# A decode attention block: half of the value products shared between VectorE and ScalarE, and a weight load cut by rows

## Chip, cores and metric

The kernel runs on one core of a Trainium2 chip. The metric is device time in microseconds for one execution. Before the change three runs gave 1308.16, 1308.84 and 1309.59 us, median 1308.84.

A core has TensorE (PE, matrix products), VectorE (DVE), ScalarE (ACT), GpSimd (POOL) and SyncE (SP, which here issues the loads). Each engine works through its own instructions in the order of the built program and waits on semaphores for the others. Sixteen DMA engines move data between memory and the core.

## The reference

One token for each of two sequences goes through an attention block with a cache and a dense block, in float32: B = 2, H = 32 heads, 8192 cached positions, head width 128, D = 512, hidden width F = 1792.

```python
# A: attention with cache
q = (x @ wq) -> [B, H, 1, 128]
scores = einsum("bhqd,bhkd->bhqk", q, k_cache) * 128**-0.5
p = softmax(scores)
o = einsum("bhqk,bhkd->bhqd", p, v_cache)
A = o.reshape(B, 1, H * 128) @ wo
# B: dense block
r = max(x @ w1 + b1, 0);  Bx = (r * r) @ w2 + b2
# whole
x = A_x
h = x + A(layernorm(x))
out = h + B(layernorm(h))
```

The two caches are 512 MiB of the 561 MB that the kernel reads.

## The kernel before

There are 64 pairs of head and sequence, here called heads 0 to 63. Each has a row of 16384 floats for each of the 128 partitions: 8192 of keys, 8192 of values, 8 MB in all. The host lays them out so that the four quarters of the positions (2048 each, `CS`) lie beside one another, and the values of a head are four columns `e` of 2048 positions (`NH = 4`), each partition holding one quarter and one of 32 widths.

`ring` in the core's memory has three slots of one head each. SyncE loads head i + 3 into the slot that head i leaves (`load_kv`). Slot 0 holds the query weights first and, at the end, the output weights `WO` (the first 16 of 32 heads of them where the keys were, the rest where the values were); slot 1 holds the dense weights `W1` and `W2` at the end.

For each head i, in this order:

- `scores` (L157 to L165): TensorE multiplies the query with the keys, 16 products of 512 columns (two passes each, so x32 in the profile), into four banks of the accumulator memory, a tile `s` of 128 x 2048. VectorE takes the negated maximum of each row into `NM` (L164).
- `exponentials` (L167 to L169): ScalarE writes exp(s - max) over `s` and sums it into `LS`.
- `weighted` (L171 to L174): for each of the four value columns one VectorE instruction multiplies the column with `s`, in place, and sums the products into `AC`. Each is followed by a short read of the accumulator.

The loop (L236 to L258) then issues the loads. Heads come in three groups, 0 to 31, 32 to 61, and 62 and 63. When a group's heads are done, `weigh` (L176 to L192) brings their maxima and sums together (L181, L183, L185, L186, L188, L189, L191), `join` (L194 to L201) gives the attention outputs `OT`, `project` (L203 to L211) multiplies them with `WO` (L207) and copies the rows by ScalarE (L210), and `add_rows` (L213 to L217) adds them to `hT`. Group 0 is joined after head 60, group 1 after head 61.

The end of the load stream is: head 61, the first half of `WO`, head 62 in two halves, head 63's keys, the second half of `WO`, head 63's values in pieces of 1 MB (three) and 512 KB (two), `W1` in four loads, `W2` in five. A load uses one of eight completion semaphores in turn, so SyncE issues a load only when the one eight before it has landed.

After the loop, head 63's values are multiplied piece by piece as they land (L287 to L295), the last heads' share of the output is added through centred weights `woc` (L308), and the dense block follows: the hidden layer `hidden` in two halves (L315) around the variance (L321) and its root `rstd` (L117), a transpose, bias and squared maximum (L329 to L334), the second layer (L337), and the store. The instruction order of each engine comes out of a scheduler that takes the program text as its starting order; `issue_after` fixes a few places.

Of the kernel before, what the change touches and what calls it, by code (L numbers as in the profile page):

```python
# [9 lines left out]
AF = mybir.ActivationFunctionType  # L10
ALU = mybir.AluOpType
AX = mybir.AxisListType

B, H, SK, DH, D, F = 2, 32, 8192, 128, 512, 1792
P = 128
NQ = 4
CS = SK // NQ
NH = DH // 32
DB = D // P
# [6 lines left out]
BLK = 512  # L26
GROUPS = [(0, 16), (16, 31), (31, 32)]
W2_PIECES = [4, 4, 3, 2, 1]
EPS = 1e-5
SCALE = DH ** -0.5  # L30

# [2 lines left out]
def attention_block_kernel(ctx: ExitStack, tc: tile.TileContext, small, kvd, wqd, wod, w1d, w2d, out):  # L34
    nc = tc.nc
# [7 lines left out]
    def slot(i):  # L43
        return ring[:, (i + 1) % SLOTS if i < BH - 2 else i - BH + 3]
# [4 lines left out]
    def values(i):  # L49
        return slot(i)[:, HALF:].rearrange("p (e c) -> p e c", e=NH)  # L50

    WQ = ring[:, 0].rearrange("p (d c) -> p d c", d=DB)
    WO = ring[:, 0].rearrange("p (h c) -> p h c", h=H)
# [3 lines left out]
    def load_kv(i):  # L57
        nc.sync.dma_start(slot(i), kvd[i])  # L58

    def load_wo(a, b):  # L60
        nc.sync.dma_start(WO[:, a:b], wod[:, a:b])
# [14 lines left out]
    eps_t = consts.tile([P, 1], F32, name="eps_t")  # L76
    nc.vector.memset(eps_t, EPS)
    zero = consts.tile([P, 1], F32, name="zero")
# [30 lines left out]
    def squares(xc):  # L109
        sq = work.tile([P, DB, B], F32, name="sq")  # L110
        nc.vector.tensor_tensor(sq, xc, xc, op=ALU.mult)
        return summed(sq)

    def scale_of(pm):

        rstd = work.tile([P, B], F32, name="rstd")
        nc.scalar.activation(rstd, pm, AF.Sqrt, bias=eps_t, scale=1.0)  # L117
        nc.vector.reciprocal(rstd, rstd)
        return rstd
# [9 lines left out]
    rstd = scale_of(bk[3][:, B : 2 * B])  # L129
# [5 lines left out]
    for k in range(2):  # L135
        for d in range(DB):
            for j in range(NQ):
                n = k * NQ + j
                nc.tensor.matmul(bk[k][32 * j : 32 * j + B, :], xn[:, d, :], WQ[:, d, n * BLK : (n + 1) * BLK],  # L139
                                 start=(d == 0), stop=(d == DB - 1))  # L140
# [13 lines left out]
    AC = consts.tile([P, BH, NH], F32, name="AC")  # L154
    OT = consts.tile([P, BH], F32, name="OT")

    def scores(i):  # L157

        s, bk = banks()
        for n in range(CS // BLK):  # L160
            for j in range(NQ):
                nc.tensor.matmul(bk[n][32 * j : 32 * j + 32, :], QR[:, i, :], keys(i)[:, j, n * BLK : (n + 1) * BLK],  # L162
                                 start=True, stop=True)
        nc.vector.tensor_reduce(NM[:, i : i + 1], s, axis=AX.X, op=ALU.max, negate=True)  # L164
        return s  # L165

    def exponentials(i, s):  # L167

        nc.scalar.activation(s, s, AF.Exp, bias=NM[:, i : i + 1], scale=1.0, accum_out=LS[:, i : i + 1])  # L169

    def weighted(i, s, e, lo, hi, acc, by=1.0):  # L171

        v = values(i)[:, e, lo:hi]
        return nc.vector.scalar_tensor_tensor(v, v, by, s[:, lo:hi], op0=ALU.mult, op1=ALU.mult, accum_out=acc)  # L174

    def weigh(a, b, pn, pl):  # L176

        nb = b - a
        pn = pn[:, : NQ * nb].rearrange("p (j i) -> p j i", j=NQ)
        for j in range(NQ):  # L180
            nc.tensor.matmul(pn[:, j], pick[:, j, :], NM[:, a:b], start=True, stop=True)  # L181
        gm = work.tile([P, BH], F32, name="gm")[:, :nb]
        nc.vector.tensor_reduce(gm, pn.rearrange("p j i -> p i j"), axis=AX.X, op=ALU.min)  # L183
        w = work.tile([P, BH], F32, name="w")[:, :nb]
        nc.vector.tensor_tensor(w, gm, NM[:, a:b], op=ALU.subtract)  # L185
        nc.scalar.activation(w, w, AF.Exp)  # L186
        lw = work.tile([P, BH], F32, name="lw")[:, :nb]
        nc.vector.tensor_tensor(lw, LS[:, a:b], w, op=ALU.mult)  # L188
        nc.tensor.matmul(pl[:, :nb], pick_all, lw, start=True, stop=True)  # L189
        rl = work.tile([P, BH], F32, name="rl")[:, :nb]  # L190
        nc.vector.reciprocal(rl, pl[:, :nb])  # L191
        return w, rl  # L192
# [26 lines left out]
    last = BH - 1  # L219
    g_at = [(a * B, b * B) for a, b in GROUPS]  # L220

    def group(n, project_now):

        a, b = g_at[n]
        _, bk = banks()
        w, rl = weigh(a, b, bk[0], bk[1])
        join(a, b, w, rl, bk[2])
        if project_now:
            clear(bk[3], D)
            add_rows(project(*GROUPS[n], bk[3]), bk[0])  # L230

    def load_half(i, half):
        cut = slice(half * HALF, (half + 1) * HALF)
        nc.sync.dma_start(slot(i)[:, cut], kvd[i][:, cut])

    for i in range(last):  # L236
        s = scores(i)
        exponentials(i, s)
        for e in range(NH):
            weighted(i, s, e, 0, CS, AC[:, i, e : e + 1])  # L240
        if i + 3 < last - 1:
            load_kv(i + 3)
        if i == last - 4:
            load_wo(0, H // 2)
        if i == last - 3:
            load_half(last - 1, 0)
            load_half(last - 1, 1)
            group(0, True)
        if i == last - 2:
            load_half(last, 0)  # L250
            load_wo(H // 2, H)
            for e in range(NH):
                n = 2 if e == NH - 1 else 1
                for k in range(n):
                    lo, hi = k * CS // n, (k + 1) * CS // n
                    at = HALF + e * CS
                    nc.sync.dma_start(values(last)[:, e, lo:hi], kvd[last][:, at + lo : at + hi])
            group(1, False)  # L258
# [3 lines left out]
    at = 0  # L262
    for n in W2_PIECES:
        nc.sync.dma_start(W2[:, at : at + n], w2d[:, at : at + n])
# [6 lines left out]
    with tc.issue_after(clear(o, P).ins):  # L271
        exponentials(last, sl)
    a, b = g_at[2]
    w, rl = weigh(a, b, sums[:, :64], sums[:, 64:128])
    nc.scalar.activation(warm, w[:, 0:1], AF.Sqrt)
    nc.vector.tensor_tensor(w, w, rl, op=ALU.mult)


    woc = work.tile([P, D], F32, name="woc")
# [19 lines left out]
        nc.tensor.matmul(po[at : at + 32, :B], fold, aw[:, :, e], start=(e < NH), stop=(e != NH - 1))  # L299
    with tc.issue_after(done.ins):  # L300
        nc.vector.tensor_copy(OT[:, a:b], po[:, :B])
    xc = work.tile([P, DB, B], F32, name="xc")
    with tc.issue_after(done.ins):
        nc.vector.tensor_tensor(xc, hT, pm[:, None, :].to_broadcast([P, DB, B]), op=ALU.subtract)
        nc.vector.tensor_tensor(hT, hT, b2T[:, :, None].to_broadcast([P, DB, B]), op=ALU.add)
    ph = sums[:, 256 : 256 + DB * B].rearrange("p (d b) -> p d b", b=B)
    for d in range(DB):
        nc.tensor.matmul(ph[:, d, :], woc[:, d * P : (d + 1) * P], OT[:, a:b], start=True, stop=True)  # L308
    nc.vector.tensor_tensor(xc, xc, ph, op=ALU.add)


    def hidden(ds):
        for d in ds:
            for j in range(NQ):
                mm = nc.tensor.matmul(y[32 * j : 32 * j + B, :], xc[:, d, :], W1[:, d, j * FQ : (j + 1) * FQ],  # L315
                                      start=(d == 0), stop=(d == DB - 1))
        return mm

    var = sums[:, 384 : 384 + B]
    with tc.issue_after(hidden(range(2)).ins):  # L320
        mm = nc.tensor.matmul(var, ones_d, squares(xc), start=True, stop=True)  # L321
    rstd = scale_of(var)
    with tc.issue_after(mm.ins):
        hidden(range(2, DB))
    for j in range(NQ):
        nc.tensor.matmul(o[32 * j : 32 * j + B, :], hT[:, j, :], ident, start=True, stop=False)  # L326
        nc.tensor.matmul(o[32 * j : 32 * j + B, :], OT[:, a:b], WO[:, H - 1, j * P : (j + 1) * P], start=False, stop=False)  # L327
# [7 lines left out]
    for m in range(FB):  # L335
        for j in range(NQ):
            nc.tensor.matmul(o[32 * j : 32 * j + B, :], a2[:, m, :], W2[:, m, j * P : (j + 1) * P],  # L337
                             start=False, stop=(m == FB - 1))
# [33 lines left out]
```

## Time and profile before

| | |
|---|---|
| median of three runs | 1308.84 us (1308.16 to 1309.59) |
| the profiled execution | 1310.04 us, span 1308.3 us |
| mean granted clock of TensorE | 0.643 |
| TensorE products busy | 417.7 us (32%) |
| VectorE busy | 728.9 us (56%) |
| ScalarE busy | 145.0 us (11%) |
| DMA | 561.44 MB in 12122 packets, mean 429 GB/s |
| issue to landing of a head's load, median | 38.8 us |

The span runs from the profiled execution's first instruction to its last; its own time is 1.7 us longer. The groups of instructions give line, engine, operation, output and inputs with shapes, count, busy time in us, mean duration in ns, and the idle time of the engine just before them with what ended most of it. The chain of waits follows back from the last instruction what released each step. Times in it and in the timeline are us from the span's start.

### The profile page before, as it was taken

The page shows a single profiled execution, that of the slowest core. Times are in us where ns is not written, and L with a number is a line of the kernel's source. Part 1 is how long each engine was busy: PE and PEld are TensorE (multiplying, and loading weights), DVE is VectorE, ACT ScalarE, POOL GpSimd, SP SyncE. Part 2 cuts the span into 40 slices and gives each one's busy share as a digit, 9 for nine tenths or more (in the row PEclk, how much of TensorE's full clock was granted, in tenths as well). Part 3 has the DMA queues.
Part 4 walks back from the last instruction along what each step waited for, and adds up shares of the span by engine and source line. Part 5 has one row for each costly group of instructions (what it writes and reads, how often), then busy time and mean ns, then how long its engine had stood idle before and what let it go on. Part 6 is the DMA issues. An engine that isn't in the chain of part 4 may idle for free.

```text
span 1308.3 us, 6011 instructions
## 1 busy us (share of the span) xinstructions
PE 417.7 (32%) x2438; PEld 114.7 (9%) x2438; DVE 728.9 (56%) x626; ACT 145.0 (11%) x152; POOL 0.7 (0%) x6
## 2 busy tenths in 40 slices
PE   2423223323323323322322332332332332332446
PEld 0100000000000000000000000000000000000113
DVE  0464665564565565565566466556456556556553
ACT  1111011011011011011101101101101101101111
POOL 0000000000000000000000000000000000000000
PEclk9666667566656666666656666756665665665766
DMA  9999999999999999999999999999999999999997
GB/s 417 417 447 425 439 433 431 441 425 443 425 439 423 441 429 435 433 435 432 433 431 435 430 437 431 435 431 433 431 437 429 437 429 437 428 439 429 426 426 313
DMA packets 12122, 561.44 MB, mean 429 GB/s; under 512 B 1472, under 2 KB 1600, under 8 KB 2752
## 3 DMA queue, kind: packets, MB, share of 16 engines
q1 hardware_dynamic: 11952, 561.06, 99.3%
q8 instruction: 19, 0.31, 0.1%
q14 instruction: 7, 0.06, 0.0%
q10 hardware_dynamic: 144, 0.01, 0.0%
HBM read 561.00 MB, written 0.07 MB: 429 GB/s over the span
## 4 chain that ended last, share of the span: by engine, by line
DMA 62%; DVE 20%; PE 12%; ACT 4%; another core or an unknown queue 1%; issue 1%; SPq 0%; ACTq 0%
DMA ring<-in_kvd 62%; DVE ring L174 16%; PE s L162 11%; DVE NM L164 4%; ACT s L169 4%; PE s L315 0%; PE s L337 0%; PE s L308 0%; DVE yT L329 0%; PE s L189 0%; PE s L321 0%; PE s L327 0%; SPq L58 0%; PE s L326 0%
## 5 line engine op out<-in xcount | busy, mean ns | idle before, releaser
L162 PE MATMUL s<-ring,QR 128*32 128x512 f32 x2048 | 373.1, 895 | 827.1 <-DMA ring<-in_kvd 718.9
L174 DVE SCALAR_TENSOR_TENSOR ring<-ring,s 128x2048 f32<-128x2048 f32 x252 | 561.5, 2284 | 133.6 <-ACT s L169 133.6
L164 DVE TENSOR_REDUCE NM<-s 128x1 f32<-128x2048 f32 x64 | 146.6, 2291 | 383.4 <-PE s L162 383.4
L169 ACT ACTIVATE s<-s,NM 128x2048 f32<-128x2048 f32 x64 | 124.3, 1942 | 1072.5 <-DVE NM L164 1072.5
L162 PEld LDWEIGHTS s<-ring,QR 128*32 128x32 f32 x2048 | 93.3, 156 | 1104.4 <-issue 1100.9
L174 DVE DVE_READ_ACCUMULATOR ring<-ring,s 128x1 f32 x252 | 20.9, 83 | 0.0
L99 DVE TENSOR_REDUCE part<-sm 128x2 f32<-128x8 f32 x1 | 0.2, 160 | 21.9 <-DMA sm<-in_small 21.9
L169 ACT ACTIVATION_READ_ACCUMULATOR s<-s,NM 128x1 f32 x64 | 12.3, 193 | 0.0
L139 PE MATMUL s<-ring,xn 128*2 128x512 f32 x64 | 9.5, 749 | 1.5 <-ACT rstd L117 0.8
L174 DVE SCALAR_TENSOR_TENSOR ring<-ring,w,s 128x2048 f32<-128x2048 f32 (+1 forms) x5 | 9.6, 1916 | 0.6 <-DMA ring<-in_kvd 0.4
L207 PE MATMUL s<-ring,OT 128*2 128x512 f32 x62 | 8.5, 682 | 3.8 <-DMA ring<-in_wod 3.5
L148 DVE TENSOR_SCALAR QR<-s 128x2048 f32<-128x2048 f32 x1 | 2.3, 2291 | 12.4 <-PE s L146 12.4
L104 PE MATMUL s<-part,ones_d 128*128 128x2 f32 x2 | 0.6, 348 | 23.2 <-DVE hT L132 23.2
L189 PE MATMUL s<-lw,pick_all 128*128 128x32 f32 (+2 forms) x6 | 1.9, 393 | 14.9 <-DVE lw L188 14.9
L315 PE MATMUL s<-ring,xc 128*2 128x448 f32 x32 | 6.3, 942 | 0.6 <-ACT rstd L117 0.4
L181 PE MATMUL s<-NM,pick 128*128 128x32 f32 (+2 forms) x24 | 4.0, 309 | 7.1 <-DVE hT L217 4.6
L95 ACT ACTIVATE s<-zero 128x512 f32<-128x512 f32 (+2 forms) x6 | 3.2, 538 | 19.8 <-DVE OT L201 10.7
L337 PE MATMUL s<-ring,a 128*2 128x128 f32 x112 | 4.7, 348 | 1.5 <-DVE a L334 1.5
L181 PEld LDWEIGHTS s<-NM,pick 128*128 128x128 f32 x24 | 3.7, 236 | 8.9 <-issue 8.9
L117 ACT ACTIVATE rstd<-s,eps_t 128x2 f32<-128x2 f32 x2 | 0.5, 262 | 32.1 <-PE s L128 20.0
L337 PEld LDWEIGHTS s<-ring,a 128*2 128x2 f32 x112 | 3.3, 107 | 3.1 <-DVE a L334 2.0
L340 DVE COPY res<-s 128x128 f32<-128x128 f32 x1 | 0.3, 292 | 4.9 <-PE s L337 4.9
(74 smaller groups left out, 45.3 us busy)
## 6 DMA issues: line engine op xcount, KB each, us to landing
ring<-in_kvd SPq DMA_DIRECT2D x3, 4096.0 KB, 32.4
ring<-in_wod SPq DMA_DIRECT2D x2, 4096.0 KB, 41.8
ring<-in_w1d SPq DMA_DIRECT2D x4, 896.0 KB, 20.3
ring<-in_kvd SPq DMA_DIRECT2D x3, 1024.0 KB, 38.2
ring<-in_w2d SPq DMA_DIRECT2D x2, 1024.0 KB, 16.2
ring<-in_kvd SPq DMA_DIRECT2D x2, 512.0 KB, 38.0
ring<-in_kvd SPq DMA_DIRECT2D x62, 38.8
ring<-in_w2d SPq DMA_DIRECT2D x1, 768.0 KB, 16.8
```

What stands on the lines that cost most here:

```text
L95: return nc.scalar.activation(ap, zero.to_broadcast([P, n]), AF.Copy)
L139: nc.tensor.matmul(bk[k][32 * j : 32 * j + B, :], xn[:, d, :], WQ[:, d, n * BLK : (n + 1) * BLK], start=(d == 0), stop=(d == DB - 1))
L148: nc.vector.tensor_scalar(QR, bk[2][:, :BH, None].to_broadcast([P, BH, 32]), SCALE, None, op0=ALU.mult)
L162: nc.tensor.matmul(bk[n][32 * j : 32 * j + 32, :], QR[:, i, :], keys(i)[:, j, n * BLK : (n + 1) * BLK], start=True, stop=True)
L164: nc.vector.tensor_reduce(NM[:, i : i + 1], s, axis=AX.X, op=ALU.max, negate=True)
L169: nc.scalar.activation(s, s, AF.Exp, bias=NM[:, i : i + 1], scale=1.0, accum_out=LS[:, i : i + 1])
L174: return nc.vector.scalar_tensor_tensor(v, v, by, s[:, lo:hi], op0=ALU.mult, op1=ALU.mult, accum_out=acc)
L181: nc.tensor.matmul(pn[:, j], pick[:, j, :], NM[:, a:b], start=True, stop=True)
L189: nc.tensor.matmul(pl[:, :nb], pick_all, lw, start=True, stop=True)
L207: nc.tensor.matmul(hp[32 * j : 32 * j + B, :], OT[:, h * B : (h + 1) * B], WO[:, h, :], start=(h - h0 < NQ), stop=(h1 - h <= NQ))
L315: mm = nc.tensor.matmul(y[32 * j : 32 * j + B, :], xc[:, d, :], W1[:, d, j * FQ : (j + 1) * FQ], start=(d == 0), stop=(d == DB - 1))
L337: nc.tensor.matmul(o[32 * j : 32 * j + B, :], a2[:, m, :], W2[:, m, j * P : (j + 1) * P], start=False, stop=(m == FB - 1))
```

## The change

Four edits.

1. For heads 0 to 61, value columns 0 and 1 are multiplied with `s` by one VectorE instruction over both columns (4096 elements a partition, `s` read twice), in place and without a sum. ScalarE then copies each product column onto itself and sums it into `AC`. Columns 2 and 3 stay as before, as do heads 62 and 63.
2. The load of the first half of `WO`, 128 rows of 32 KB, becomes four loads of 112, 12, 2 and 2 rows.
3. At the end, the products with `woc` are written ahead of the two VectorE operations on `xc` and `hT`.
4. `rstd` is written behind the second half of the hidden layer.

```diff
+WO_ROWS = [112, 12, 2, 2]
...
+    def shared(i, s):
+
+        v = values(i)[:, : NH // 2]
+        nc.vector.tensor_tensor(v, v, s[:, None, :].to_broadcast([P, NH // 2, CS]), op=ALU.mult)
+        for e in range(NH // 2):
+            nc.scalar.activation(v[:, e], v[:, e], AF.Copy, accum_out=AC[:, i, e : e + 1])
...
-        for e in range(NH):
+        if i < last - 1:
+            shared(i, s)
+        for e in range(NH // 2 if i < last - 1 else 0, NH):
             weighted(i, s, e, 0, CS, AC[:, i, e : e + 1])
...
         if i == last - 4:
-            load_wo(0, H // 2)
+            lo = 0
+            for n in WO_ROWS:
+                nc.sync.dma_start(WO[lo : lo + n, : H // 2], wod[lo : lo + n, : H // 2])
+                lo += n
...
+    ph = sums[:, 256 : 256 + DB * B].rearrange("p (d b) -> p d b", b=B)
+    for d in range(DB):
+        nc.tensor.matmul(ph[:, d, :], woc[:, d * P : (d + 1) * P], OT[:, a:b], start=True, stop=True)
     xc = work.tile([P, DB, B], F32, name="xc")
     with tc.issue_after(done.ins):
         nc.vector.tensor_tensor(xc, hT, pm[:, None, :].to_broadcast([P, DB, B]), op=ALU.subtract)
         nc.vector.tensor_tensor(hT, hT, b2T[:, :, None].to_broadcast([P, DB, B]), op=ALU.add)
-    ph = sums[:, 256 : 256 + DB * B].rearrange("p (d b) -> p d b", b=B)
-    for d in range(DB):
-        nc.tensor.matmul(ph[:, d, :], woc[:, d * P : (d + 1) * P], OT[:, a:b], start=True, stop=True)
...
-    rstd = scale_of(var)
     with tc.issue_after(mm.ins):
         hidden(range(2, DB))
+    rstd = scale_of(var)
```

In the built program one more thing moves on TensorE. Before: head 61's scores, the projection of group 0 (L207, L216), group 1's sums (L181, L189, L200), head 62's scores. After (line numbers of the changed kernel): head 61's scores, group 1's sums (L189, L197, L208), the projection of group 0 (L215, L224), head 62's scores. The orders of the other engines follow it.

## The prediction

> **What bounds the kernel now.** I read the page first, parts 2 and 3.
>
> ```profile
> DMA  9999999999999999999999999999999999999997
> ...
> q1 hardware_dynamic: 11952, 561.06, 99.3%
> q8 instruction: 19, 0.31, 0.1%
> q14 instruction: 7, 0.06, 0.0%
> ```
>
> The DMA row is full in every slice but the last: the kernel streams 561 MB and waits for them. Two thin queues, q8 and q14, fetch instructions on the same DMA engines. Then the groups, for what one head's 8 MB (every 19.36 us) costs in compute:
>
> ```profile
> L174 DVE SCALAR_TENSOR_TENSOR ring<-ring,s 128x2048 f32<-128x2048 f32 x252 | 561.5, 2284 | 133.6 <-ACT s L169 133.6
> L164 DVE TENSOR_REDUCE NM<-s 128x1 f32<-128x2048 f32 x64 | 146.6, 2291 | 383.4 <-PE s L162 383.4
> L169 ACT ACTIVATE s<-s,NM 128x2048 f32<-128x2048 f32 x64 | 124.3, 1942 | 1072.5 <-DVE NM L164 1072.5
> ```
>
> VectorE, the busiest, idles for TensorE's scores or ScalarE's exponentials, 517 us in all. Only the end can be compute-bound, so I asked for the chain of waits there (start, length, what):
>
> ```profile
> 1217.83 8.92 DVE ring L174 x8
> ...
> 1228.34 5.34 PE s L162 x32
> ...
> 1244.86 38.45 DMA ring<-in_kvd
> 1283.30 0.02 issue
> 1283.33 0.49 DVE ring L174
> ```
>
> From landing to free slot a head takes 19 us (1207.9 to 1226.7) while two more loads, 39 us, are queued: in the loop compute has 20 us to spare. At the end the third value piece of head 63 lands at 1283.30 and decides. The timeline shows how little the compute chain lags behind (the bracket is the idle time before and its releaser):
>
> ```profile
> 1247.18 1.89 PE L181 MATMUL s<-NM,pick 128*128 128x30 f32 x8 [4.62 <-DVE hT L217]
> ...
> 1251.35 5.83 PE L162 MATMUL s<-ring,QR 128*32 128x512 f32 x32
> ...
> 1271.54 2.29 DVE L164 TENSOR_REDUCE NM<-s 128x1 f32<-128x2048 f32 x1 [0.82 <-PE s L162]
> ...
> 1278.35 2.35 DVE L174 SCALAR_TENSOR_TENSOR ring<-ring,w,s 128x2048 f32<-128x2048 f32 x1 [0.36 <-DMA ring<-in_kvd]
> ...
> 1295.03 3.17 PE L315 MATMUL s<-ring,xc 128*2 128x448 f32 x16 [0.35 <-ACT rstd L117]
> ```
>
> VectorE waits 0.36 us for the first value piece: compute is ready at 1277.99, almost with the data. Two chains end together, and both must be priced.
>
> Last, the trace's single packets. Every engine moves one 64 KB row in 2.42 us (32 KB: 1.22), back to back. The 16 completion marks of a load drift apart: head 60's come from 1202.7 to 1207.9. Seven engines are within 0.8 us of the first, eight 1.6 to 3.5 behind, one 5.2. Each 16 KB fetch (q8) holds one engine up by 1.5 us (1.05 gap, next row 2.9 instead of 2.42), rotating over eight engines; five of the seven 8 KB fetches (131, 384, 617, 869, 1122 us) hit one and the same engine, 0.97 us each (0.31 + 0.66), and so make the laggard. q8 comes every 77.5 us, four heads of 64 TensorE records: 64 bytes an instruction. VectorE runs 10 instructions a head (reduce, four multiplies, four accumulator reads, one semaphore wait): 128 of them last 12.8 heads, 248 us, and the five come 247.7 us apart. The laggard carries VectorE's code.
>
> **The change, part by part.**
>
> *Shared multiply, heads 0 to 61.* On VectorE two multiplies (2.21 us start to start, reads hidden) become one over 4096 columns. The trace has none that long: nearest are twice the 2048 row, 4.42, and the slope of the small tensor-tensors (128 columns 0.28, 32 columns 0.19: 0.94 ns a column, 4.0 in all). I take 4.42: no gain; ends -0.4 and +0.2 a head. ScalarE adds two copies with sums, 2.07 us each like exp with its read: 4.14 beside VectorE's two remaining multiplies, 4.43. Slots come free when they do now, and ScalarE's next exp is 10 us off. In the loop the price is nought, under 20 us of cover. At the end heads 60 and 61 are on the chain: 0, ends -0.8 and +0.4.
>
> *Instruction stream.* VectorE falls to 7 a head (reduce, product, one wait, two multiplies, two reads): a fetch per 18.3 heads or 354 us, three before head 60 instead of five. The laggard falls to 0.4 + 3 x 0.97 = 3.3 us, below the 3.5 of the eight. ScalarE rises from 2 to 7: three fetches. The other two 8 KB fetches hit two other engines now within 0.8 us, where 2.9 more still fits. Head 60 then lands 5.2 - 3.5 = 1.75 us earlier. Ends: -1.75, and +1.0 if ScalarE's fetches share the laggard (six for five). I take -1.75: the fetches that miss the laggard show separate engines.
> [...]
>
> *TensorE's order.* The built program moves head group 0's projection (L215, L224 after) behind group 1's sums. Now it sits between heads 61 and 62 and fills the wait for VectorE. In the old clock, group 1's gm no longer waits for it: 1247.0 instead of 1249.1; its sums end at 1249.4. Then come the projection (3.61 us warm; the later one took 4.88 for 15 heads from cold: 5.2 for 16), copy 0.75, add 1.1, and only then head 62's scores: 1256.5. TensorE is warm by then, 0.43 a step, 3.45 us: they end at 1260.0 instead of 1257.2. Reduce, exp, four multiplies: head 63's reduce at 1273.5 instead of 1271.54, past its 0.82 us of slack: +2.0. Ends +1.5 and +3.
>
> *WO in four loads.* Three more DMAs on SyncE, 0.35 us issue each, with data queued 20 us ahead: nothing. Head 63's first pieces also wait for ScalarE's copies of head 61 (1244.6, 1246.7 instead of 1240.4): covered, the queue lasts to 1275.9. No run shows how 112, 12 or 2 rows spread. Bounds: as evenly as now (0), or all 16 leftover rows on one engine, (7 + 16 - 8) x 1.22 = 18.3 us there. I take 0, as every load shown spreads evenly.
> [...]
>
> *Tail.* L317's matmuls (L308 before, idle 0.32 us until xc) now follow OT alone (-0.1), the second half of the hidden layer no longer for rstd (-0.35): -0.45.
>
> *Sum.* Compute chain, first piece: 1277.99 + 2.0 - 1.75 = 1278.25; third piece two steps of 2.27 later, 1282.8. Data: third piece lands behind the engines with a third 16 KB fetch, 4.9 us late instead of 5.2: 1283.0. So 1283.0 for 1283.33, -0.3; with the tail -0.75. The second layer's last weights land at 1303.3 and are used at 1304.9: covered. The profiled execution took 1310.04 (span 1308.3), 1.2 over the median of 1308.84; I carry the difference over: 1308.84 - 0.75 = 1308.1.
>
> **The rivals.**
>
> *No relief in the stream.* If ScalarE's fetches join VectorE's, head 60 lands 0 to 1.0 later. First piece 1280.0 to 1281.0, third 1284.5 to 1285.5: +1.2 to +2.2, less 0.45: 1309.6 to 1310.6. For it: both are q14. Against: two fetches hit other engines.
>
> *Slower: the short loads crowd engines that lag.* Decided from the point where an engine lags more than 5.2 us at head 63's pieces. [...] All leftovers on one free engine: 18.3 + 0.8 - 5.2 = +13.9, 1322. For it: eight of sixteen engines lag already. Against: seven are nearly free, and three rows fit there.
>
> *Slower: the long multiply runs at half rate*, 8.8 us: +4.4 at heads 60 and 61 each, +8 at the end, 1316. Nothing in the rows asks for it.
>
> [...]
>
> **How the numbers follow.** Forecast 0.50; no relief 0.17; crowding 0.17 (0.05 of it the extreme); half rate 0.04; order cheaper 0.08; 0.04 for something in the stream that I do not see. The range takes the forecast with half a microsecond of scatter, the faster case, the relief rival and mild crowding: 1306.9 to 1310.9. A change under 0.2%, 2.6 us, is about what a measurement of this kernel can tell from none; most cases lie inside: same 0.75. Slower 0.17: extreme crowding, half rate, unseen stream loss, and parts of the relief and crowding rivals that add up. Faster 0.08: the faster case with all its ends.
>
> **What would show it.** Right: 4.4 us for the long multiply; q14 fetches on the laggard 354 us apart and head 60's marks spread over 3.5 us; head 62's scores about 5 us after the old place relative to head 61's landing, ending 3 us later; no wait for rstd in the hidden layer. Wrong: a spread over 5.2 us at head 63's pieces, or VectorE waiting over 0.4 us for them.

## The result: 15.5 us slower, and the profile after

The changed kernel takes 1324.01 us (median of four, 1323.41 to 1325.1) against 1308.51 beside it: a ratio of 1.0119, 95% interval 1.0106 to 1.0131. Forecast were 1308.1 us and no change. The profiled execution took 1324.44 us, span 1322.7.

The page of the changed kernel, parts 2, 3 and 5 (for the groups: busy us, mean ns of one, idle before):

```profile
GB/s 413 437 420 440 438 423 437 440 425 434 440 426 432 440 428 431 438 431 428 440 431 428 440 430 431 438 429 435 434 431 436 433 430 438 431 430 433 235 426 322
...
q14 instruction: 10, 0.08, 0.0%
...
L180 DVE TENSOR_TENSOR ring<-ring,s 128x4096 f32<-128x4096 f32 x62 | 274.1, 4421 | 131.3 <-ACT s L170 131.3
L182 ACT ACTIVATE ring<-ring 128x2048 f32<-128x2048 f32 x124 | 235.7, 1901 | 278.1 <-DVE ring L180 278.1
```

The line of rates on the page before the change:

```profile
GB/s 417 417 447 425 439 433 431 441 425 443 425 439 423 441 429 435 433 435 432 433 431 435 430 437 431 435 431 433 431 437 429 437 429 437 428 439 429 426 426 313
```

The rate holds at about 433 GB/s through all 62 heads that share their products. One slice of 33 us, near the end, has 235, where the same slice before had 426. That slice is nearly the whole loss: (433 - 235) x 33 / 433 = 15.1 us. The same place in windows of 10 us (the last three columns are TensorE's clock, the busy share of the DMA engines and GB/s):

```profile
1220.00:1230.00 10.00, 0.97 (x10) 0.70 (x10) 7.35 (x9) 4.50 (x5) 0.00 (x0) 0.50 1.01 256
1230.00:1240.00 10.00, 6.55 (x32) 1.61 (x32) 2.29 (x1) 0.51 (x1) 0.00 (x0) 0.67 1.05 223
1240.00:1250.00 10.00, 0.00 (x0) 0.00 (x0) 8.42 (x4) 5.44 (x6) 0.00 (x0) 0.50 0.96 191
1250.00:1260.00 10.00, 7.85 (x46) 3.39 (x49) 1.81 (x8) 0.23 (x1) 0.00 (x0) 0.50 0.96 408
```

The DMA engines are as busy as ever, share 0.96 to 1.05, and move about half as much for 30 us, 191 to 256 GB/s. So nothing starves them: each packet takes longer. The trace's single packets say which: the first 128 rows of 32 KB, nearly all of them rows of `WO`'s first half, take 2.42 us in the mean, where before they took 1.22, and the last rows of head 61, which lagging engines still write while the others have gone on to `WO`, up to 4.95 instead of 2.42. The chain of waits then runs over the loads:

```profile
1186.81 43.60 DMA ring<-in_kvd
...
1230.55 6.59 PE s L163 x32
...
1251.38 47.16 DMA ring<-in_kvd
...
1298.56 1.83 DVE ring L175
```

Head 61 lands at 1230.4 instead of 1227.3, and the third value piece of head 63 at 1298.5 instead of 1283.3.

### The profile page after: what moved, and what is told of

It is laid out like the page before. It is cut to its first block, busy times and chain, and to the rows that moved or that the text cites. A ratio compares the mean times of both kernels' runs of the same rounds, so it can differ in the third digit from the quotient of the medians.

```text
span 1322.7 us, 6200 instructions
## 1 busy us (share of the span) xinstructions
PE 410.6 (31%) x2438; PEld 113.1 (9%) x2438; DVE 723.7 (55%) x440; ACT 386.5 (29%) x400; POOL 0.7 (0%) x6
## 4 chain that ended last, share of the span: by engine, by line
DMA 66%; DVE 18%; PE 11%; issue 3%; another core or an unknown queue 1%; ACT 0%; SPq 0%
DMA ring<-in_kvd 66%; PE s L163 10%; DVE ring L175 7%; DVE ring L180 7%; DVE NM L165 4%; PE s L328 0%; PE s L350 0%; ACT s L170 0%; PE s L317 0%; SPq L59 0%; SPq L270 0%; DVE yT L342 0%; PE s L334 0%; SPq L62 0%
## 5 line engine op out<-in xcount | busy, mean ns | idle before, releaser
L163 PE MATMUL s<-ring,QR 128*32 128x512 f32 x2048 | 361.8, 870 | 844.6 <-DMA ring<-in_kvd 791.1
L180 DVE TENSOR_TENSOR ring<-ring,s 128x4096 f32<-128x4096 f32 x62 | 274.1, 4421 | 131.3 <-ACT s L170 131.3
L182 ACT ACTIVATE ring<-ring 128x2048 f32<-128x2048 f32 x124 | 235.7, 1901 | 278.1 <-DVE ring L180 278.1
L175 DVE SCALAR_TENSOR_TENSOR ring<-ring,s 128x2048 f32<-128x2048 f32 x128 | 287.2, 2281 | 2.6 <-DMA ring<-in_kvd 2.6
L182 ACT ACTIVATION_READ_ACCUMULATOR ring<-ring 128x1 f32 x124 | 23.1, 186 | 0.0
L215 PE MATMUL s<-ring,OT 128*2 128x512 f32 x62 | 12.8, 978 | 0.3 <-DVE rl L199 0.3
L175 DVE DVE_READ_ACCUMULATOR ring<-ring,s 128x1 f32 x128 | 10.6, 83 | 0.0
L189 PE MATMUL s<-NM,pick 128*128 128x32 f32 (+2 forms) x24 | 4.0, 309 | 16.0 <-DVE ring L175 13.5
L197 PE MATMUL s<-lw,pick_all 128*128 128x32 f32 (+2 forms) x6 | 1.9, 394 | 14.9 <-DVE lw L196 14.9
L189 PEld LDWEIGHTS s<-NM,pick 128*128 128x128 f32 x24 | 3.7, 237 | 19.2 <-issue 19.2
```

Of the source, the lines that this page charges most:

```text
L180: nc.vector.tensor_tensor(v, v, s[:, None, :].to_broadcast([P, NH // 2, CS]), op=ALU.mult)
L182: nc.scalar.activation(v[:, e], v[:, e], AF.Copy, accum_out=AC[:, i, e : e + 1])
L215: nc.tensor.matmul(hp[32 * j : 32 * j + B, :], OT[:, h * B : (h + 1) * B], WO[:, h, :], start=(h - h0 < NQ), stop=(h1 - h <= NQ))
```

## The experiments

Four theories were tried first. **A**: the short loads of `WO` stall the stream. **B**: the shared products cost the time. **C**: TensorE's new order costs it. **D** (first set): more loads, with semaphores in turn, cost it. All edits below are to the kernel before unless said otherwise.

**The changed kernel with one WO load.**

```diff
-            lo = 0
-            for n in WO_ROWS:
-                nc.sync.dma_start(WO[lo : lo + n, : H // 2], wod[lo : lo + n, : H // 2])
-                lo += n
+            load_wo(0, H // 2)
```

> The changed kernel with its four WO loads put back to one of 128 rows; the shared products and both tail edits stay, and TensorE's order is the old one again. Theory A (the row split stalls the load stream): no stall, head 60 lands 1.4 us earlier than before, the end is set by the value pieces: 1307.8 us, between 1307.0 and 1308.5. Theory B (the shared products cost the time, by ScalarE's traffic or the slots): 1322 to 1324 us as in the changed kernel. Theory C (TensorE's new order costs it): also 1307.8, so the third run is needed to part A from C.

Measured 1308.20 us against 1308.57, ratio 0.9997 (0.9988 to 1.0006). B falls: sharing 62 heads costs nothing that can be told, and the slow part sits in edit 2 or in what the scheduler makes of it.

**Only the short loads, TensorE's order held.**

```diff
-            load_wo(0, H // 2)
+            lo = 0
+            for n in [112, 12, 2, 2]:
+                nc.sync.dma_start(WO[lo : lo + n, : H // 2], wod[lo : lo + n, : H // 2])
+                lo += n
...
-            group(1, False)
+            with tc.issue_after(added.ins):
+                group(1, False)
```

(`added` is the last product of group 0's `add_rows`.)

> The kernel before with nothing but the four WO loads of 112, 12, 2 and 2 rows; group 1's sums are held behind group 0's projection, so TensorE's order stays as before. Theory A: 32 KB rows take 2.4 us instead of 1.22, the rate falls to half for some 25 us, the third value piece of head 63 lands near 1298 instead of 1283: 1322 to 1325 us. Theories B and C: 1308.5 us, no stall.

Measured 1324.99 us, ratio 1.0125 (1.0111 to 1.0139); the rows take 2.53 us. A holds alone: the loss is there without sharing, without the tail and without the new order.

**Only the order.** `group` hands back its banks, and group 0's projection is written behind group 1's sums:

```diff
-            group(1, False)
+            _, mm = group(1, False)
+            with tc.issue_after(mm.ins):
+                add_rows(project(*GROUPS[0], bk0[3]), bk0[0])
```

> The kernel before with one WO load, but group 0's projection moved behind group 1's sums on TensorE, as in the changed kernel. Theory A: the load stream is untouched; head 62's scores start about 12.6 us after head 61's last multiply (1247.0) instead of 4.3, end near 1263.5 instead of 1257.2, and the third value piece is multiplied about 5 us later: 1313 us (1311 to 1315). The step of the prediction (+2.0, less slack) would give 1310. Theory C: 1322 to 1324 us.

Measured 1312.78 us, ratio 1.0033 (1.0020 to 1.0045): 4.2 us, as expected from the changed kernel's trace and not what the prediction had summed. The chain of waits of this run:

```profile
1239.73 8.93 DVE ring L174 x8
...
1248.80 1.90 PE s L181 x8
...
1253.24 5.84 PE s L208 x32
...
1260.92 3.65 PE s L162 x30
...
1264.59 2.30 DVE NM L164
```

Group 1's first product (L181) comes only when head 61's last multiply is over (1248.7), and the projection (L208 here) runs 5.84 us. Head 62's scores end at 1264.6 instead of 1257.2, and now compute, not the stream, sets the end. In the changed kernel these 4 us lie under the 15 of the stall, so the two don't add.

**Four loads over all partitions**, as a control for the number of loads:

```diff
-            load_wo(0, H // 2)
+            for h in range(0, H // 2, 4):
+                load_wo(h, h + 4)
```

> The kernel before with the first half of WO in four loads of 128 rows and four heads each (8 KB a row) instead of one: the same number of loads as the changed kernel, but each over all partitions. Theory A: full rate, 8 KB rows in 0.31 us, the value pieces land as before, 1308 to 1310 us. Theory D (more loads, and semaphores in turn, stall the stream): a dip in the rate as in the changed kernel, over 1315 us.

Measured 1308.32 us, one run. The page's rates show no dip:

```profile
GB/s 418 427 438 419 446 421 444 423 443 424 441 428 435 436 429 437 428 439 426 439 427 438 430 436 431 434 432 435 432 433 434 431 436 431 436 429 437 417 426 337
```

D falls: four loads are as good as one if each has 128 rows (1308.32 against 1308.57).

**What in the rows does it?** The next runs keep TensorE's order held and change only the list of rows. One run each: the verdict rests on the row times in the packets and on the rate, not on the time to a tenth. Three theories are here. **U**: an uneven split makes single engines lag. **P**: the partitions that a load covers set its pace. **Q**: any load of fewer than 128 rows runs at half pace. For 64 and 64 the author's estimate under P and under Q was twice the 1.22 us a row, 9.7 us lost over eight rows an engine, 1317 to 1319 us. First, 64 and 64:

```diff
-            for n in [112, 12, 2, 2]:
+            for n in [64, 64]:
```

> The kernel before with the first half of WO in two loads of 64 rows; TensorE's order as before. Every engine still carries eight 32 KB rows, so the split is even. Theory U (uneven rows make single engines lag): no loss, 32 KB rows in 1.22 us, 1308 to 1309 us. [...]

Measured 1326.93 us against 1308.37, and 2.52 us a row. The packets of the kernel before and of the changed one show 128 and 112 rows spread evenly, eight and seven in each of sixteen chains. With 64 rows spread in the same way the split is even, and yet the rows run at half pace, on all engines: U falls, the uneven split is not the cause. The loss, 18.6 us, is nearly twice what P and Q gave. They counted `WO`'s own 128 rows. In this run, as in all of these, some 160 rows of 32 KB are slow, not 128; the rest belong to head 62, and ten rows of head 61 are slow too. Together that is 14.2 us an engine; the other 4 us of this single run are not accounted for.

The packets also say when the slow pace ends. They don't name their engine, but rows that follow one another without a gap fall into sixteen chains. The engines lag behind one another, so while some still write `WO`, others carry head 61 or head 62. Rows on all engines are slow from about `WO`'s first row to about its last (1221.7 to 1253.0; in the changed kernel 1222.0 to 1251.4), a little less so near the end, and the rows that start after it take 1.22 us again. The rates of this run's page:

```profile
GB/s 412 442 423 430 441 433 428 437 438 423 434 440 425 434 439 434 429 432 437 433 428 437 430 433 434 431 435 438 429 434 435 426 435 437 428 429 410 264 423 286
```

Then eight loads of 16, `[16] * 8`:

> The kernel before with the first half of WO in eight loads of 16 neighbouring rows; TensorE's order as before, one row an engine and load. Theory U: no loss, 1308 to 1309 us. Theory Q: 2.43 us a row, 1317 to 1319 us. Theory P: rows slower than in the loads of 64, and more time lost. [...]

Measured 1334.64 us and 3.52 us a row. Q falls: 16 neighbouring partitions a load give slower rows than 64 (3.52 us against 2.52). Some of the time here is SyncE's waiting between its issues, five waits of 3.0 to 3.4 us in the chain from 1242 to 1260, so it is the row time that counts. The page:

```profile
GB/s 410 439 441 426 427 437 437 439 419 437 435 437 431 431 429 439 439 427 429 435 437 433 433 429 441 429 431 431 439 427 435 433 437 433 429 431 345 205 422 309
```

And 112 and 16 rows, `[112, 16]`:

> The kernel before with the first half of WO in two loads of 112 and 16 rows; TensorE's order as before. Both counts are multiples of 16, so every engine can carry seven rows and one. Theory U: no loss, 1308 to 1309 us. Theories P and Q: the stall of the changed kernel comes from the 112 rows themselves, 2.3 to 2.5 us a row, 9 to 15 us lost, 1317 to 1324 us; the loads of 12, 2 and 2 rows add the rest up to its 1325.

Measured 1325.94 us, above the 1317 to 1324 expected, and 2.52 us a row, as with 112, 12, 2 and 2: loads of 112 and 16 rows are enough, and the smaller ones add nothing that shows. It also says that the count of partitions alone doesn't set the pace: 112 are no faster than 64 (2.52 us both).

**Written or read?** The last three runs have eight loads of 16 rows again, seven of which take every seventh partition, every seventh row of memory, or both. Theory **D** is here: the partitions written decide; **M**: the rows read decide.

```diff
+            for lo in range(7):
+                nc.sync.dma_start(WO[lo:112:7, : H // 2], wod[16 * lo : 16 * lo + 16, : H // 2])
+            nc.sync.dma_start(WO[112:, : H // 2], wod[112:, : H // 2])
```

> As the run with eight loads of 16 rows, but seven of the eight go to every seventh partition (0, 7, 14 and so on) instead of 16 neighbours; the rows read are the same 16 neighbouring ones, so the first half of WO lies in other partitions and the output is not the reference's. [...] Theory Q (only the small count of rows an engine matters): as there.

Measured 1326.60 us, 2.62 us a row. The mirror, `WO[16 * lo : 16 * lo + 16]` from `wod[lo:112:7]`:

> The mirror: seven loads read every seventh row of WO but write 16 neighbouring partitions; the first half of WO lies in other partitions and the output is not the reference's. Theory D: no better than the run with eight loads of 16 neighbours, 3.2 to 3.8 us a row, 1332 to 1337 us. Theory M: faster, 1316 to 1323 us. Theory Q: 1332 to 1336 us.

Measured 1333.30 us, 3.54 us a row. Both spread:

> Seven loads of 16 rows that read and write every seventh row and partition, and one of the last 16: nothing is permuted. Theory D: as with spread partitions alone, 1316 to 1323 us. Theory M: also 1316 to 1323. Theory Q: 1332 to 1336 us.

Measured 1325.15 us, 2.49 us a row. The rates of the slice with the dip (last four slices of each page): 414 233 424 320 with both spread, 409 234 423 317 with the writes spread, 344 186 429 329 with the reads spread. Spreading the writes takes the row from 3.5 to 2.6 us whatever is read; spreading the reads does nothing (3.52 and 3.54). These three ran on another chip than the runs before them, so the comparison that counts is among them: 2.62 and 2.49 against 3.54. M falls. D holds as to what decides, but not in size: the rows stay above the 1.2 to 2.4 us of the author's estimate, and 1326.6 and 1325.2 us lie above its 1316 to 1323.

**Only the shared products.** One load, the old tail, the old order.

> The kernel before with nothing but the shared products: one WO load, the old tail, the old order. Theory A: instruction fetches of VectorE fall from five to three on the laggard, head 60's marks spread over 3.5 us instead of 5.2, the value pieces land 0.4 us earlier: 1308.0 us, not to be told from before. Against the run with the tail edits (1308.2): if these had saved 0.45 us, this would be 1308.6; the profile there shows the waits only moved, so 1307.9 to 1308.2. Theory B (sharing costs time): over 1311 us.

Measured 1308.35 us against 1308.37, ratio 1.0000 (0.9991 to 1.0009). No version beat the kernel before by more than can be told.

The row times side by side, mean of the first 128 rows of 32 KB (117 to 120 of them `WO`'s, the rest head 62's):

| loads of WO's first half (rows each) | us a row | time |
|---|---|---|
| 128 (before) | 1.22 | 1308.5 |
| 112, 12, 2, 2 (changed kernel) | 2.42 | 1324.0 |
| 112, 12, 2, 2 alone | 2.53 | 1325.0 |
| 112, 16 | 2.52 | 1325.9 |
| 64, 64 | 2.52 | 1326.9 |
| 16 x 8, neighbours | 3.52 | 1334.6 |
| 16 x 8, reads spread | 3.54 | 1333.3 |
| 16 x 8, writes spread | 2.62 | 1326.6 |
| 16 x 8, both spread | 2.49 | 1325.2 |

## Why the prediction was wrong

**The step that failed is "WO in four loads ... I take 0, as every load shown spreads evenly".** Both its bounds counted rows per engine: as even as now, or all the leftovers on one engine. Neither allowed that a row itself could take twice as long, because every row in the trace of before was part of a load of 128. An operation that no row shows in its shape (here a load over fewer partitions) had been priced by rows of another shape. The runs showed a row time of 2.4 to 2.5 us on all engines at once, and a slow pace that takes some 35 more rows of head 62 and the last of head 61 with it: in the changed kernel's packets (4.73 - 2.42) x 11 rows of 64 KB and (2.48 - 1.22) x 164 of 32 KB make 25 + 207 us over sixteen engines, 14.5 us each. The 1322 of the extreme in the crowding rival came near the time by luck, by another mechanism; the 64 and 64 run, with eight rows on every engine, rules that mechanism out.

The split itself was uneven. In the trace of the changed kernel the load of 12 rows has 13 completion marks and those of 2 rows have 3 each, where every other load has 16 (1363 in all, 1344 before); and of the sixteen chains of rows two carry ten rows of `WO`, ten carry eight and four carry seven. It decided nothing that shows: the first seven rows of `WO` took 2.34 to 2.53 us in the mean on every one of the sixteen chains, and the even 64 and 64 lost more. The range of the forecast also took in a faster case, with lagging engines relieved by 1.2 us, and a mild crowding of such engines. No run shows either term; the runs showed all sixteen engines slow in their place, 14.5 us each in the changed kernel.

P fits in part. The 2.52 us of 64 and 64 are twice 1.22, and 16 neighbours are slower still, 3.52. But the splits with 112 neighbours took 2.42 to 2.53, about as much as 64, and sixteen rows seven apart 2.49 to 2.62. So the count of partitions that a load covers is not the whole cause of the changed kernel's loss.

**TensorE's order** was priced at +2.0 on the compute chain and costs 4.2 us at the end of its own run. The step that failed is "group 1's gm no longer waits for it: 1247.0". It still waits, because the product before it (L181 before, L189 in the changed kernel) starts only when head 61's multiplies end. In the changed kernel, idle before and its releaser in brackets:

```profile
1250.56 1.89 PE L189 MATMUL s<-NM,pick 128*128 128x30 f32 x8 [13.46 <-DVE ring L175]
1252.49 0.28 DVE L191 TENSOR_REDUCE gm<-s 128x30 f32<-128x120 f32 x1 [2.07 <-PE s L189]
...
1262.97 3.64 PE L163 MATMUL s<-ring,QR 128*32 128x512 f32 x32
```

Why this product waits for those multiplies is not shown. The projection, too, ran longer than taken in the run with the order alone, 5.84 us for 5.2. The warm clock for head 62's scores came as forecast (3.64 us for 3.45, at a granted clock of 1.00).

**The shared products** were right term by term: 4.421 us for the long multiply (4.42), 1.90 plus 0.19 for a copy and its read (2.07), slots free on time.

**The instruction stream** was right too. In the run with one `WO` load head 60's marks spread over 3.5 us and it lands at 1206.1, 1.8 us earlier than before (1.75), and at 1206.0 in the run with only the shared products. VectorE's fetches come 350 us apart (354), and ten 8 KB fetches instead of seven hold up other engines harmlessly.

**The tail** gained nothing: -0.45 was the wrong sign for one edit and a moved wait for the other. In the changed kernel:

```profile
1305.94 0.16 DVE L320 TENSOR_TENSOR xc<-hT,s 128x8 f32<-128x8 f32 x1 [1.96 <-PE s L317]
...
1306.43 3.17 PE L328 MATMUL s<-ring,xc 128*2 128x448 f32 x16 [0.53 <-DVE xc L322]
...
1312.53 0.26 ACT L118 ACTIVATE rstd<-s,eps_t 128x2 f32<-128x2 f32 x1 [13.31 <-PE s L328]
...
1312.85 0.42 PE L339 MATMUL s<-ident,hT 128*2 128x128 f32 x8 [0.39 <-ACT rstd L118]
```

`xc`, written behind the products, now waits for them, and three VectorE steps follow instead of one (0.53 us idle). And `rstd` now waits for the whole hidden layer, so that TensorE waits 0.39 us for it one step later.

One more step of the prediction failed here: that the second layer's last weights are covered. In the run with one `WO` load the chain of waits ends with them:

```profile
1285.37 16.80 DMA ring<-in_w2d
1302.16 0.04 issue
1302.21 0.62 PE s L347 x16
```

The run with four loads by columns, otherwise the kernel before, ends in the same way (the weights land at 1302.6). The profile that the prediction read, 1310.04 us, had a slower tail: the second half of its hidden layer took 3.17 us at a granted clock of 0.50, against 1.69 us at 1.00 in the run by columns. So in that profile compute set the end, and in these two faster executions (1308.1 and 1308.3 us) the stream did. There neither a value piece that lands earlier nor a shorter tail can show beyond what the last weights gain.

Without the split and without the new order (the run with one `WO` load), the other parts give 1308.20 for 1308.57, -0.4 where -0.75 was forecast, and not to be told from nothing.

**Settled and open.** That the short loads carry the whole loss, that the loss is there without sharing and without the new order, and that an even split doesn't help, was shown. That the partitions written and not the rows read set the pace, and that four loads do no harm if each has 128 rows, rests on one run each, whose row times lie far apart. What it is in the partitions stays open: 112 neighbours, 64 neighbours and 16 spread ones all take about 2.5 us a row. One rival is untested: a split may also change which engine writes which partition, and the packets name neither.

## What to carry to other kernels

In a kernel bound by its stream, price a load by a row measured in its own shape, not by its bytes or its engines: 4 MB over 128 partitions cost 9.7 us of the stream, the same bytes in pieces of 112, 64 or 16 partitions some 24 to 34 us, by estimate from the rows that were slow. To cut a load, cut its columns: that run lost nothing (1308.32 us, one run). Look at the rate slice by slice: the DMA busy row stayed full here while the rate fell to 235 GB/s, and a single dip of 33 us held everything.

## What the runs showed of the hardware that was not expected

- The loads over 112, 64 or 16 partitions slowed all sixteen engines, also those that carried rows of the neighbouring loads over 128: 64 KB rows of head 61 took up to 4.95 us instead of 2.42 beside them in the changed kernel (up to 7.6 beside the loads of 16). The slowing lasted about from the first row of such loads to the last, and ended with them (1222.0 to 1251.4 us in the changed kernel).
- Instruction fetches were not free in this full stream: in the trace of before each 8 KB fetch of VectorE held one DMA engine up by 0.97 us (0.31 for itself, 0.66 on the next row), and with three fewer instructions a head, in the run with one `WO` load, head 60 landed 1.8 us earlier.
